# Score tiles on VectorE from the first slots on: 139 tiles instead of 94, with borrowed buffers and projections laid out by need

## The chip, the cores and the metric

The kernel runs on one core of one Trainium2 chip. The metric is the device time of one execution in microseconds (us). Executions of one kernel on one chip usually agree within 0.3%. All runs quoted are "fast" (none was over 1.5% above the fastest run of its kernel). Engine names in the profile: PE is TensorE's matmuls, PEld its weight loads, DVE is VectorE, ACT is ScalarE, POOL is GpSimd.

## The reference

```python
def reference(A_x, A_wqkv, A_w_phi, A_wo, B_x, B_wqkv, B_wo, gate_w):
    x = A_x                                            # 1 x 2048 x 512, 32 heads of 16
    g = sigmoid((x * gate_w).sum(-1, keepdims=True))
    a = linear_attention(x, A_wqkv, A_w_phi, A_wo)     # feature maps by softmax over 16
    b = softmax_attention(x, B_wqkv, B_wo)             # full 2048 x 2048 scores per head
    return g * a + (1 - g) * b
# ... (cut: the two blocks in full)
```

The softmax block needs 32 x 2048 x 2048 exponentials. Cut into tiles of 128 x 512 these are 2048 tiles. The linear block ("A" in names) is much smaller, and runs in the gaps.

## The kernel before

The program is a list of operations with planned durations and priorities. A list scheduler in the kernel's own Python lays them out once, at build time; each engine then executes its fixed order, and semaphores hold the dependences. One *slot* is three score tiles in three of the eight accumulation banks. ScalarE exponentiates all three, or two of them while VectorE does the third by a bit trick and a cubic (six operations). Two sets of three banks alternate, one bank holds the attention output, and one bank (`bM`) serves everything else. A *projection* is the matmuls that compute a piece of Q, K, V or the like into `bM`; the *drain* is the copy out of the bank afterwards, mostly by VectorE, and only then is `bM` free again. *Value products* multiply the exponentials by V.

```python
D_FROM, D_MID, D_RATE = 200, 420, (0.14, 0.25)    # VectorE tiles per slot: 0, then 0.14, then 0.25
# ... (cut)
def add_qk(j):                                    # scores of slot j
    def fn(e):
        if op.full > 0.3:                         # a dummy matmul ahead of the scores
            e.matmul(psS[:, 512 * base:512 * (base + 1)], lhsT=ident[:], rhs=WoA[:, 0, :], start=True, stop=True)
        for m, t in enumerate(ts):
            ins = qk_mm(e, t, psS[:, 512 * (base + m):512 * (base + m + 1)])
# ... (cut)
def add_exp(j):                                   # ScalarE: 1536 or 1024 columns
    op = P.add("act", ..., lambda e: e.activation(Ebuf[:, j % ERING, 0:512 * n],
        psS[:, 512 * base:512 * (base + n)], ACTF.Exp, bias=EBIAS, scale=ESCALE), ...)
# ... (cut) in the scheduler: PE work that the layout thinks PE owes, to keep it active
if op.name[:2] == "qk" and debt > self.inslot and t > 240.0:
    op.full = 0.42                                # this score group gets its dummy
```

When PE would otherwise have nothing to do and `bM` is free, the layout also puts "filler" dummies there. Dummies compute nothing; they keep PE active.

The softmax here doesn't subtract the row's maximum and nothing guards it: scores larger than these inputs give would overflow.

Of the kernel before, what the change touches and what calls it, by code (L numbers as in the profile page):

```python
# [13 lines left out]
S = 2048  # L14
# [19 lines left out]
DLAG = 10  # L34
D_FROM = 200
D_MID = 420
D_RATE = (0.14, 0.25)
ERING = 8
LAT = 0.12
# [38 lines left out]
class Plan:  # L78
# [37 lines left out]
    def layout(self):  # L116
# [16 lines left out]
        while left:  # L133
# [26 lines left out]
            for e in ENGINES:  # L160
# [39 lines left out]
                if e == "pe":  # L200
                    if op.name[:2] == "qk" and debt > self.inslot and t > 240.0:
                        op.full = 0.42
                        op.dur += 0.28
                    debt = max(debt - op.full, -0.2)
# [89 lines left out]
def _build(ctx, nc, A_x, A_wqkv, A_w_phi, A_wo, B_wqkv, B_wo, gate_w, out):  # L294
# [22 lines left out]
    phiK = sb([128, 8, 1024], name="phiK")  # L317
    Ebuf = sb([128, ERING, 1536], name="E")
    Pf = sb([128, 2, D], F32, name="Pf")
# [185 lines left out]

    def q_fill(r, qc, prio, banks=None, first=False):
        f, mm = fill(prio, proj([W_B[:, t, 128 * r:128 * (r + 1)] for t in range(KT)],
                                [xT[:, t, NQ * qc:NQ * (qc + 1)] for t in range(KT)]), ["wbq" if r else "wbq0"] + xk(qc), banks,
                     name=f"Q{r}.{qc}")
        for par in range(2):  # L510
            dst = qz[:, qc % 2, 2 * r + par, :]
            if first and par == 0:
                fn = lambda e, ap, dst=dst: e.activation(dst, ap, ACTF.Copy, scale=pmask[:, 0:1])
            else:
                fn = lambda e, ap, dst=dst, par=par: e.tensor_scalar(dst, ap, pmask[:, par:par + 1], None,  # L515
                                                                     op0=ALU.mult)
            e1 = drain(f, mm, "act" if first and par == 0 else "dve", 0.69, prio, fn, reads=["pmask"],
                       writes=[("q", qc % 2, 2 * r + par)], name=f"Qe{r}.{qc}.{par}", last=(par == 1),
                       after=[e1] if par == 1 else ())


    def d_rate(j):
        return 0.0 if j < D_FROM else D_RATE[0] if j < D_MID else D_RATE[1]

# [58 lines left out]
    for act, _ in slots:  # L583
        for t in act:
            last_act[t[0]] = t
    d_index = {j: n for n, (j, _) in enumerate(tiles_d)}
    ND = len(tiles_d)
    vfree = vAf[:, 0:8192].bitcast(F32).rearrange("p (n c) -> p n c", c=1024)
    I32 = mybir.dt.int32
    dT = [vfree[:, 0, :], vfree[:, 1, :]]  # L590
    dM, dU = vfree[:, 2, :], vfree[:, 3, :]
    dE = [W_B[:, t, D:3 * D] for t in range(KT)]

    exp_ops = [None] * NS
    pv_last = []
    d_wait = []

# [7 lines left out]
    def add_qk(j):  # L605
# [19 lines left out]
        if j == 1:  # L625
            op.take = [bS[3], bS[4], bS[5]]
        if j == 60:
            op.deps += P.writer["WoA"]
# [4 lines left out]
    def add_d(j, bank):  # L633

        n = d_index[j]
        bt, half = (n // 2) % 2, n % 2
        be = (n // 2) % 4
        free = (va_free + kv_mm) if n < 2 else ()
        P.add("dve", 0.72, -45, lambda e: e.tensor_scalar(  # L639
            dT[bt].bitcast(I32)[:, 512 * half:512 * half + 512], bank, EXPB, 0.0, op0=ALU.add, op1=ALU.max),  # L640
            reads=[("S", j % 2)], writes=[("dT", bt, half)], after=free, name=f"D1.{n}")
        if half == 0 and n + 1 < ND:
            return
        w = 512 * (half + 1)
        keys = [("dT", bt, h) for h in range(half + 1)]
        t, m, u = dT[bt][:, 0:w], dM[:, 0:w], dU[:, 0:w]
        P.add("dve", 0.75 * w / 1024, -20, lambda e: e.tensor_scalar(  # L647
            m.bitcast(I32), t.bitcast(I32), 0x007FFFFF, 0x3F800000, op0=ALU.bitwise_and, op1=ALU.bitwise_or),
            reads=keys, writes=["dM"], name=f"D2.{n}")
        P.add("dve", 0.75 * w / 1024, -20, lambda e: e.tensor_single_scalar(  # L650
            t.bitcast(I32), t.bitcast(I32), 0x7F800000, ALU.bitwise_and), reads=keys + ["dM"], writes=keys,
            name=f"D3.{n}")
        P.add("dve", 1.25 * w / 1024, -20, lambda e: e.scalar_tensor_tensor(u, m, C2, m, op0=ALU.add, op1=ALU.mult),  # L653
              reads=["dM"], writes=["dU"], name=f"D4.{n}")
        P.add("dve", 1.25 * w / 1024, -20, lambda e: e.scalar_tensor_tensor(u, u, C1, m, op0=ALU.add, op1=ALU.mult),  # L655
              reads=["dM", "dU"], writes=["dU"], name=f"D5.{n}")
        P.add("dve", 1.25 * w / 1024, -20, lambda e: e.scalar_tensor_tensor(  # L657
            dE[be][:, 0:w], u, C0, t, op0=ALU.add, op1=ALU.mult), reads=["dU"] + keys, writes=[("dE", be)],
            name=f"D6.{n}")

# [19 lines left out]
    def add_pv(j):  # L680
# [4 lines left out]
        for b, mts in parts.items():  # L685
# [7 lines left out]
            for x in list(d_wait):  # L693
                jd, n, t = x
                if t[0] != b or (b, t[1]) not in pv_started:
                    continue
                if last or (jd + DLAG <= j and t[1] not in heads):
                    d_wait.remove(x)
                    heads.append(t[1])
                    work.append((t, dE[(n // 2) % 4][:, 512 * (n % 2):512 * (n % 2) + 512], False))  # L700
                    if ("dE", (n // 2) % 4) not in reads:
                        reads.append(("dE", (n // 2) % 4))
            for t, _, _ in work:
# [12 lines left out]
            op.full = 0.21  # L716
            pv_last.append(op)
            if j == 0:
                op.take = [bO]
            if first:  # L720
                op.margin = 1.0
            if last:
                assert not [x for x in d_wait if x[2][0] == b]
                add_norm(b, op)
        if dt:
            d_wait.append((j, d_index[j], dt))

# [170 lines left out]
    def q_rest(i, prio):  # L898
# [7 lines left out]
        for rnd in range(2):  # L906
# [10 lines left out]
                  writes=[("dr", b, rnd)], name=f"nb{i}.{rnd}")  # L917
            P.add("dve", 0.38, -3, lambda e, dr=dr: e.tensor_scalar(dr, dr, g128[:, i:i + 1], None, op0=ALU.mult),
                  reads=[("dr", b, rnd), "g128"], writes=[("dr", b, rnd)], name=f"nc{i}.{rnd}")
# [36 lines left out]
    for r in range(1, KT):  # L956
        q_fill(r, 0, 57.0 * r - 15)
        for c in range(QC):
            k_fill(r, c, 57.0 * r - 14 + 6 * c)
            v_fill(r, c, 57.0 * r - 13 + 6 * c)  # L960
    gate()
# [17 lines left out]
    for j in range(NS):  # L979
        add_exp(j)  # L980
        if j + 2 < NS:
            add_qk(j + 2)
        add_pv(j)
        b1 = slots[j][0][-1][0]
        while q_next < NB and q_next // 8 >= 1 and q_next // 2 * 2 - 8 < b1:
            q_fill(q_next % 8 // 2, q_next // 8, 20.0 * q_next - 30)
            q_next += 2
    for j in (NS - 2, NS - 1):
        exp_ops[j].rel = [bS[3 * (j % 2) + m] for m in range(3)]

    P.idle = (bM, 0.05, lambda e: e.matmul(psM[:], lhsT=ident[:], rhs=WoA[:, 0, :], start=True, stop=True),  # L991
# [35 lines left out]
```

## Time and profile before

938.24 us median of 3 runs (937.41 to 938.62) when the prediction was made.

Lines of the page of the kernel before: busy time (share) and instructions by engine; busy tenths in 40 slices; the chain that ended last.

```profile
PE 810.6 (86%) x5807; PEld 253.5 (27%) x5908; DVE 595.1 (64%) x927; ACT 913.2 (97%) x720; POOL 142.0 (15%) x131
...
DVE  2436565457454787777856765476776776766774
ACT  6999999999999999999999999999999999999996
...
PEclk9999999999989999899999999999999999999999
...
ACT 91%; PE 6%; DVE 3%; issue 0%
```

Groups of instructions of the kernel before, ScalarE alone, shapes kept apart (busy us, mean ns of one | idle before).

```profile
L664 ACT ACTIVATE E_t<-psS 128x1536 bf16<-128x1536 f32 x588 | 815.7, 1572 | 7.9 <-PE psS L601 7.6
L664 ACT ACTIVATE E_t<-psS 128x1024 bf16<-128x1024 f32 x95 | 104.7, 1102 | 0.6 <-PE psS L601 0.6
L857 ACT ACTIVATE EA_t<-Dd_t 128x1024 bf16<-128x1024 bf16 x32 | 40.4, 1263 | 0.0
```

ScalarE is the bound: busy 97%, 91% of the chain. The recorded durations of successive exponentials overlap, so the useful number is the *pitch*, start to start. Reading the starts one by one, an undisturbed 1536-wide exponential has a pitch of 1330 ns, a 1024-wide one of 903, the linear block's (EA_t) of 946. "Idle before" (8.5 us for these two groups) shows less than half of the waiting, 19.7 us by pitch: the rest lies inside the records. I therefore use an account of my own throughout: the span is the head (to the first exponential), plus the sum of these undisturbed pitches, plus the excess of each real pitch over its undisturbed one, plus the tail. The excess is split into what lies within 1.5 us of a stretch where the clock records show half speed, what follows a short (1024-wide) exponential, and the rest. For the kernel before: 10.9 + 897.3 + (11.2 + 5.2 + 3.3) + 9.3 = 937.2 us.

### The profile page before, as it was taken

How to read it: one execution, taken by the hardware profiler on the slowest of the kernel's cores; microseconds unless marked ns; L12 is line 12 of the kernel's file. 1: busy time of each engine (PE TensorE's matmuls, PEld its weight loads, DVE VectorE, ACT ScalarE, POOL GpSimd, SP SyncE). 2: the span in 40 equal slices, each digit the busy share in tenths (PEclk: the TensorE clock that was granted, in tenths of full speed). 3: DMA queues.
4: the chain of work that ended last, by engine and by line, in shares of the span. 5: the costliest groups of instructions: out<-in, count | busy, mean ns of one | idle time of the engine just before them, and what ended most of it. 6: DMA issues, size and time to landing. Idle time of an engine off the chain costs nothing.

```text
span 937.2 us, 13684 instructions
## 1 busy us (share of the span) xinstructions
PE 810.6 (86%) x5807; PEld 253.5 (27%) x5908; DVE 595.1 (64%) x927; ACT 913.2 (97%) x720; POOL 142.0 (15%) x131
## 2 busy tenths in 40 slices
PE   8887888887888888888788888888999998899998
PEld 3232323322322222222222222222222222222222
DVE  2436565457454787777856765476776776766774
ACT  6999999999999999999999999999999999999996
POOL 5004334325321221400401200000000000000000
PEclk9999999999989999899999999999999999999999
DMA  7500000000000000000000000000000000000000
GB/s 147 124 2 1 1 1 1 1 1 1 1 7 12 1 7 1 1 2 1 1 1 1 18 7 1 1 1 1 1 1 1 17 6 1 1 1 1 1 1 23
DMA packets 18956, 9.28 MB, mean 10 GB/s; under 512 B 13264, under 2 KB 18896, under 8 KB 18896
## 3 DMA queue, kind: packets, MB, share of 16 engines
q1 hardware_dynamic: 16928, 8.00, 3.5%
q8 instruction: 46, 0.75, 0.3%
q10 hardware_dynamic: 1584, 0.39, 0.2%
q0 software_dynamic: 384, 0.02, 0.1%
q14 instruction: 14, 0.11, 0.0%
HBM read 3.69 MB, written 2.10 MB: 6 GB/s over the span
## 4 chain that ended last, share of the span: by engine, by line
ACT 91%; PE 6%; DVE 3%; issue 0%
ACT E_t L664 88%; ACT EA_t L857 3%; PE psS L601 1%; PE psO L677 1%; PE psM L479 1%; PE psS L619 1%; PE psM L395 1%; DVE stat_t L861 0%; PE psM L991 0%; DVE qz_t L515 0%; DVE rd_t L736 0%; DVE Wp_t L825 0%; DVE Tf_t L731 0%; DVE vA_t L647 0%; DVE Pf_t L842 0%
## 5 line engine op out<-in xcount | busy, mean ns | idle before, releaser
L664 ACT ACTIVATE E_t<-psS 128x1536 bf16<-128x1536 f32 (+1 forms) x683 | 890.3, 1507 | 8.5 <-PE psS L601 8.2
L601 PE MATMUL psS<-qz_t,kTB_t 32*128 32x512 bf16 x2048 | 272.7, 391 | 47.3 <-ACT E_t L664 38.5
L677 PE MATMUL psO<-E_t,vaug_t 128*32 128x512 bf16 (+1 forms) x1954 | 270.4, 398 | 1.0 <-ACT E_t L664 0.4
L619 PE MATMUL psS<-WoA_t,ident_t 128*128 128x512 bf16 x244 | 97.5, 399 | 51.2 <-ACT E_t L664 46.6
L639 DVE TENSOR_SCALAR vA_t<-psS 128x512 int32<-128x512 f32 x94 | 64.6, 687 | 113.2 <-PE psS L601 113.2
L601 PEld LDWEIGHTS psS<-qz_t,kTB_t 32*128 32x128 bf16 x2048 | 66.5, 91 | 239.9 <-ACT E_t L664 155.8
L677 PEld LDWEIGHTS psO<-E_t,vaug_t 128*32 128x32 bf16 (+1 forms) x1954 | 64.9, 93 | 154.4 <-issue 138.1
L991 PE MATMUL psM<-WoA_t,ident_t 128*128 128x512 bf16 x278 | 89.4, 385 | 2.0 <-issue 1.9
L851 POOL TENSOR_TENSOR Dd_t<-Pf_t,stat_t 128x512 bf16<-128x512 f32 x32 | 33.8, 1057 | 242.7 <-DVE stat_t L846 232.9
L619 PEld LDWEIGHTS psS<-WoA_t,ident_t 128*128 128x128 bf16 x274 | 26.5, 97 | 123.2 <-ACT E_t L664 115.1
L655 DVE SCALAR_TENSOR_TENSOR vA_t<-vA_t 128x1024 f32<-128x1024 f32 x47 | 57.1, 1216 | 0.8
L657 DVE SCALAR_TENSOR_TENSOR WB_t<-vA_t 128x1024 bf16<-128x1024 f32 x47 | 57.1, 1215 | 0.8
L653 DVE SCALAR_TENSOR_TENSOR vA_t<-vA_t 128x1024 f32<-128x1024 f32 x47 | 57.0, 1213 | 0.0
L842 DVE COPY Pf_t<-psM 128x512 f32<-128x512 f32 x32 | 21.9, 685 | 43.3 <-PE psM L479 41.3
L861 DVE TENSOR_REDUCE stat_t<-EA_t 128x64 f32<-128x1024 bf16 x32 | 38.7, 1212 | 15.2 <-ACT EA_t L857 15.1
L865 POOL TENSOR_TENSOR phiQ_t<-EA_t,stat_t 128x1024 bf16<-128x1024 bf16 x16 | 31.4, 1967 | 81.9 <-DVE stat_t L863 81.9
L479 PE MATMUL psM<-Wp_t,xT_t 128*128 128x512 bf16 x115 | 36.0, 384 | 6.3 <-DVE vA_t L834 3.4
L857 ACT ACTIVATE EA_t<-Dd_t 128x1024 bf16<-128x1024 bf16 x32 | 40.4, 1263 | 0.0
L865 POOL TENSOR_TENSOR phiK_t<-EA_t,stat_t 128x1024 bf16<-128x1024 bf16 x16 | 30.8, 1928 | 53.7 <-DVE stat_t L863 46.0
L479 PE MATMUL psM<-xT_t,WB_t 128*128 128x512 bf16 x107 | 34.0, 396 | 4.5 <-issue 1.3
L677 PE MATMUL psO<-WB_t,vaug_t 128*32 128x512 bf16 (+1 forms) x94 | 37.3, 396 | 0.0
L647 DVE TENSOR_SCALAR vA_t<-vA_t 128x1024 int32<-128x1024 int32 x47 | 34.3, 730 | 1.2
(102 smaller groups left out, 581.0 us busy)
## 6 DMA issues: line engine op xcount, KB each, us to landing
out_dram<-WvA_t SPq DMA_DIRECT2D x16, 128.0 KB, 1.7
WB_t<-in_B_wqkv_dram SPq DMA_DIRECT2D x3, 384.0 KB, 4.3
Dd_t<-in_A_x_dram SPq DMA_DIRECT2D x4, 128.0 KB, 3.4
WvA_t<-in_A_wqkv_dram SPq DMA_DIRECT2D x1, 512.0 KB, 5.3
WoA_t<-in_A_wo_dram SPq DMA_DIRECT2D x1, 512.0 KB, 6.2
WoB_t<-in_B_wo_dram SPq DMA_DIRECT2D x1, 512.0 KB, 6.6
WB_t<-in_B_wqkv_dram ACTq DMA_DIRECT2D x3, 128.0 KB, 3.8
xT_t<-in_A_x_dram SPq DMA_TRANSPOSE x12, 4.0
```

The costliest lines, as they stand in the source:

```text
L479: return [lambda e, ap, i=i: e.matmul(ap, lhsT=lhs[i], rhs=rhs[i], start=(i == 0), stop=(i == len(lhs) - 1)) for i in range(len(lhs))]
L601: return e.matmul(bank, lhsT=kT_B[32 * i:32 * i + 32, hg // 2, 128 * kt:128 * (kt + 1)], rhs=qz[32 * i:32 * i + 32, (b // 8) % 2, hg, :], ...
L619: e.matmul(psS[:, 512 * base:512 * (base + 1)], lhsT=ident[:], rhs=WoA[:, 0, :], start=True, stop=True)
L639: P.add("dve", 0.72, -45, lambda e: e.tensor_scalar(dT[bt].bitcast(I32)[:, 512 * half:512 * half + 512], bank, EXPB, 0.0, op0=ALU.add, op1 ...
L653: P.add("dve", 1.25 * w / 1024, -20, lambda e: e.scalar_tensor_tensor(u, m, C2, m, op0=ALU.add, op1=ALU.mult), reads=["dM"], writes=["dU"] ...
L655: P.add("dve", 1.25 * w / 1024, -20, lambda e: e.scalar_tensor_tensor(u, u, C1, m, op0=ALU.add, op1=ALU.mult), reads=["dM", "dU"], writes= ...
L657: P.add("dve", 1.25 * w / 1024, -20, lambda e: e.scalar_tensor_tensor(dE[be][:, 0:w], u, C0, t, op0=ALU.add, op1=ALU.mult), reads=["dU"] + ...
L664: op = P.add("act", 0.07 + 0.000833 * 512 * n, 0.0, lambda e: e.activation(Ebuf[:, j % ERING, 0:512 * n], psS[:, 512 * base:512 * (base + ...
L677: return e.matmul(psO[32 * i:32 * i + w, :], lhsT=vaug[:, kt, VW * h:VW * h + w], rhs=rhs, start=start, stop=stop, tile_position=(0, 32 * ...
L857: ex = P.add("act", 1.2, -4, lambda e: e.activation(EA[:, b, :], Dd[:, b, :], ACTF.Exp), reads=[("D", b, 0), ("D", b, 1)], writes=[("EA", ...
L865: P.add("pool", 2.0, prio, lambda e: e.tensor_tensor(dst.rearrange("p (g f) -> p g f", f=DH), e3, stat[:, b, 1, :].unsqueeze(2).to_broadca ...
L991: P.idle = (bM, 0.05, lambda e: e.matmul(psM[:], lhsT=ident[:], rhs=WoA[:, 0, :], start=True, stop=True), P.writer["WoA"][0])
```

## The change

Its intent: let VectorE take score tiles also in the first 200 slots. The buffers of the late tiles are still in use then, so an early pool borrows those of the linear block's query pass, which has to wait for the last early tile. More tiles late as well. Projections of K, V and Q are laid out by when they are needed, and dummies inside score groups may come from 60 us on, not 240. Cut to the core:

```diff
-D_FROM = 200
-D_MID = 420
-D_RATE = (0.14, 0.25)
-ERING = 8
+D_RATE = ((14, 0.15), (196, 0.0), (222, 0.17), (420, 0.31))
+D_SWITCH = 210
+ERING = 7
@@ scheduler
-                    if op.name[:2] == "qk" and debt > self.inslot and t > 240.0:
+                    if op.name[:2] == "qk" and debt > self.inslot and t > 60.0:
@@ buffers of VectorE tiles
+    dp_early = DPool("a", 512, [f32(phiQ[:, 0, :]), f32(phiQ[:, 1, :])], f32(qtf[:, 0, :]), f32(qtf[:, 1, :]),
+                     [oA[:, 0, :], oA[:, 1, :]] + [Ebuf[:, ERING, 512 * k:512 * k + 512] for k in range(3)], ())
+    dp_late = DPool("b", 1024, [vfree[:, 0, :], vfree[:, 1, :]], vfree[:, 2, :], vfree[:, 3, :],
+                    [W_B[:, t, D:3 * D] for t in range(KT)], (va_free, kv_mm))
@@ projections
-        q_fill(r, 0, 57.0 * r - 15)
+        q_fill(r, 0, 34.0 * r - 20)
         for c in range(QC):
-            k_fill(r, c, 57.0 * r - 14 + 6 * c)
-            v_fill(r, c, 57.0 * r - 13 + 6 * c)
+            k_fill(r, (c - 1) % QC, 34.0 * r - 19 + 3 * c)
+        for c in range(QC):
+            v_fill(r, c, 34.0 * r - 7 + 4 * c)
@@ (cut: planned durations, a cheaper denominator scaling, and the query pass's wait for the early tiles)
```

The number of slots stays 683. By the instructions of the program, 94 VectorE tiles become 139 (27 early, 112 late), and dummies go from 274 in score groups and 308 fillers to 403 and 90.

More of the change, by code (lines that the diff above doesn't have):

```diff
@@ L317, in _build @@
     phiK = sb([128, 8, 1024], name="phiK")
-    Ebuf = sb([128, ERING, 1536], name="E")
+    Ebuf = sb([128, ERING + 1, 1536], name="E")
     Pf = sb([128, 2, D], F32, name="Pf")
@@ L504, in v_fill, with q_fill @@
             dst, ap.rearrange("p (i h d) -> p i h d", i=4, d=DH)), writes=[("v", r, c)], name=f"Ve{r}.{c}")
-    def q_fill(r, qc, prio, banks=None, first=False):
+    def q_fill(r, qc, prio, banks=None, first=False, after=()):
         f, mm = fill(prio, proj([W_B[:, t, 128 * r:128 * (r + 1)] for t in range(KT)],
                                 [xT[:, t, NQ * qc:NQ * (qc + 1)] for t in range(KT)]), ["wbq" if r else "wbq0"] + xk(qc), banks,
-                     name=f"Q{r}.{qc}")
+                     name=f"Q{r}.{qc}", after=after)
         for par in range(2):
@@ L522, in d_rate @@
     def d_rate(j):
-        return 0.0 if j < D_FROM else D_RATE[0] if j < D_MID else D_RATE[1]
+        return max([(j0, r) for j0, r in D_RATE if j0 <= j] + [(-1, 0.0)])[1]
     NB = QC * 8
@@ L585, in _build, with __init__, place, f32 @@
             last_act[t[0]] = t
-    d_index = {j: n for n, (j, _) in enumerate(tiles_d)}
-    ND = len(tiles_d)
-    vfree = vAf[:, 0:8192].bitcast(F32).rearrange("p (n c) -> p n c", c=1024)
-    I32 = mybir.dt.int32
-    dT = [vfree[:, 0, :], vfree[:, 1, :]]
-    dM, dU = vfree[:, 2, :], vfree[:, 3, :]
-    dE = [W_B[:, t, D:3 * D] for t in range(KT)]
+    I32 = mybir.dt.int32
+    class DPool:
+        def __init__(self, tag, w, t, m, u, e, free):
+            self.tag, self.w, self.t, self.m, self.u, self.e, self.free = tag, w, t, m, u, e, free
+            self.per = w // 512
+            self.n, self.ops = 0, []
+        def place(self, n):
+            k = n // self.per
+            return k % len(self.t), n % self.per, k % len(self.e)
+    def f32(ap):
+        return ap.bitcast(F32)
+    vfree = vAf[:, 0:8192].bitcast(F32).rearrange("p (n c) -> p n c", c=1024)
+    qtf = phiQT[:].rearrange("p b g q -> p b (g q)")
+    dp_early = DPool("a", 512, [f32(phiQ[:, 0, :]), f32(phiQ[:, 1, :])], f32(qtf[:, 0, :]), f32(qtf[:, 1, :]),
+                     [oA[:, 0, :], oA[:, 1, :]] + [Ebuf[:, ERING, 512 * k:512 * k + 512] for k in range(3)], ())
+    dp_late = DPool("b", 1024, [vfree[:, 0, :], vfree[:, 1, :]], vfree[:, 2, :], vfree[:, 3, :],
+                    [W_B[:, t, D:3 * D] for t in range(KT)], (va_free, kv_mm))
+    d_place = {}
+    for j, _ in tiles_d:
+        dp = dp_early if j < D_SWITCH else dp_late
+        d_place[j] = (dp, dp.n)
+        dp.n += 1
     exp_ops = [None] * NS
     pv_last = []
-    d_wait = []
+    d_wait, early_pv, early_last = [], [], []
     def qk_mm(e, t, bank):
@@ L626, in add_qk @@
             op.take = [bS[3], bS[4], bS[5]]
-        if j == 60:
+        if j == 35:
             op.deps += P.writer["WoA"]
@@ L633, in add_d @@
     def add_d(j, bank):
-        n = d_index[j]
-        bt, half = (n // 2) % 2, n % 2
-        be = (n // 2) % 4
-        free = (va_free + kv_mm) if n < 2 else ()
-        P.add("dve", 0.72, -45, lambda e: e.tensor_scalar(
-            dT[bt].bitcast(I32)[:, 512 * half:512 * half + 512], bank, EXPB, 0.0, op0=ALU.add, op1=ALU.max),
-            reads=[("S", j % 2)], writes=[("dT", bt, half)], after=free, name=f"D1.{n}")
-        if half == 0 and n + 1 < ND:
+        dp, n = d_place[j]
+        bt, half, be = dp.place(n)
@@ new lines, in add_d, with add @@
+        free = sum(dp.free, []) if n < 2 * dp.per else ()
+        def add(dur, prio, fn, reads, writes, name):
+            dp.ops.append(P.add("dve", dur, prio, fn, reads=reads, writes=[(dp.tag,) + k for k in writes],
+                                after=free, name=f"{name}.{j}"))
+        add(0.70, -45, lambda e: e.tensor_scalar(
+            dp.t[bt].bitcast(I32)[:, 512 * half:512 * half + 512], bank, EXPB, 0.0, op0=ALU.add, op1=ALU.max),
+            [("S", j % 2)], [("T", bt, half)], "D1")
@@ L643, in add_d @@
+        if half < dp.per - 1 and n + 1 < dp.n:
             return
         w = 512 * (half + 1)
-        keys = [("dT", bt, h) for h in range(half + 1)]
-        t, m, u = dT[bt][:, 0:w], dM[:, 0:w], dU[:, 0:w]
-        P.add("dve", 0.75 * w / 1024, -20, lambda e: e.tensor_scalar(
-            m.bitcast(I32), t.bitcast(I32), 0x007FFFFF, 0x3F800000, op0=ALU.bitwise_and, op1=ALU.bitwise_or),
-            reads=keys, writes=["dM"], name=f"D2.{n}")
-        P.add("dve", 0.75 * w / 1024, -20, lambda e: e.tensor_single_scalar(
-            t.bitcast(I32), t.bitcast(I32), 0x7F800000, ALU.bitwise_and), reads=keys + ["dM"], writes=keys,
-            name=f"D3.{n}")
@@ L653, in add_d @@
-        P.add("dve", 1.25 * w / 1024, -20, lambda e: e.scalar_tensor_tensor(u, m, C2, m, op0=ALU.add, op1=ALU.mult),
-              reads=["dM"], writes=["dU"], name=f"D4.{n}")
-        P.add("dve", 1.25 * w / 1024, -20, lambda e: e.scalar_tensor_tensor(u, u, C1, m, op0=ALU.add, op1=ALU.mult),
-              reads=["dM", "dU"], writes=["dU"], name=f"D5.{n}")
-        P.add("dve", 1.25 * w / 1024, -20, lambda e: e.scalar_tensor_tensor(
-            dE[be][:, 0:w], u, C0, t, op0=ALU.add, op1=ALU.mult), reads=["dU"] + keys, writes=[("dE", be)],
-            name=f"D6.{n}")
+        f1, f2 = 0.17 + 0.53 * w / 1024, 0.17 + 1.06 * w / 1024
@@ new lines, in add_d @@
+        tk = [("T", bt, h) for h in range(half + 1)]
+        rt = [(dp.tag,) + k for k in tk]
+        rm, ru = [(dp.tag, "M")], [(dp.tag, "U")]
+        t, m, u = dp.t[bt][:, 0:w], dp.m[:, 0:w], dp.u[:, 0:w]
+        add(f1, -20, lambda e: e.tensor_scalar(m.bitcast(I32), t.bitcast(I32), 0x007FFFFF, 0x3F800000,
+                                               op0=ALU.bitwise_and, op1=ALU.bitwise_or), rt, [("M",)], "D2")
+        add(f1, -20, lambda e: e.tensor_single_scalar(t.bitcast(I32), t.bitcast(I32), 0x7F800000, ALU.bitwise_and),
+            rt + rm, tk, "D3")
@@ L661, in add_exp @@
+        add(f2, -20, lambda e: e.scalar_tensor_tensor(u, m, C2, m, op0=ALU.add, op1=ALU.mult), rm, [("U",)], "D4")
+        add(f2, -20, lambda e: e.scalar_tensor_tensor(u, u, C1, m, op0=ALU.add, op1=ALU.mult), rm + ru, [("U",)], "D5")
+        add(f2, -20, lambda e: e.scalar_tensor_tensor(dp.e[be][:, 0:w], u, C0, t, op0=ALU.add, op1=ALU.mult),
+            ru + rt, [("E", be)], "D6")
     def add_exp(j):
@@ L693, in add_pv @@
             for x in list(d_wait):
-                jd, n, t = x
+                jd, t = x
                 if t[0] != b or (b, t[1]) not in pv_started:
@@ L699, in add_pv @@
                     heads.append(t[1])
-                    work.append((t, dE[(n // 2) % 4][:, 512 * (n % 2):512 * (n % 2) + 512], False))
-                    if ("dE", (n // 2) % 4) not in reads:
-                        reads.append(("dE", (n // 2) % 4))
+                    dp, n = d_place[jd]
+                    _, half, be = dp.place(n)
+                    work.append((t, dp.e[be][:, 512 * half:512 * half + 512], False))
+                    if (dp.tag, "E", be) not in reads:
+                        reads.append((dp.tag, "E", be))
+                    if dp is dp_early:
+                        early_pv.append(j)
             for t, _, _ in work:
@@ L717, in add_pv @@
             pv_last.append(op)
+            if early_pv and early_pv[-1] == j:
+                early_last[:] = [op]
             if j == 0:
@@ L722, in add_pv @@
             if last:
-                assert not [x for x in d_wait if x[2][0] == b]
+                assert not [x for x in d_wait if x[1][0] == b]
                 add_norm(b, op)
         if dt:
-            d_wait.append((j, d_index[j], dt))
+            d_wait.append((j, dt))
     def add_norm(b, pv):
@@ L917, in q_rest @@
                   writes=[("dr", b, rnd)], name=f"nb{i}.{rnd}")
-            P.add("dve", 0.38, -3, lambda e, dr=dr: e.tensor_scalar(dr, dr, g128[:, i:i + 1], None, op0=ALU.mult),
+            P.add("dve", 0.2, -3, lambda e, dr=dr: e.tensor_tensor(dr, dr, g128[:, i:i + 1].to_broadcast([128, 16]),
+                                                                   ALU.mult),
                   reads=[("dr", b, rnd), "g128"], writes=[("dr", b, rnd)], name=f"nc{i}.{rnd}")
@@ L985, in _build @@
         while q_next < NB and q_next // 8 >= 1 and q_next // 2 * 2 - 8 < b1:
-            q_fill(q_next % 8 // 2, q_next // 8, 20.0 * q_next - 30)
+            q_fill(q_next % 8 // 2, q_next // 8, -0.5, after=[exp_ops[j]])
             q_next += 2
@@ L989, in _build @@
         exp_ops[j].rel = [bS[3 * (j % 2) + m] for m in range(3)]
+    for op in P.ops:
+        if op.name in ("phi0.0", "phi0.1", "Te0", "Te1", "nd0.0", "nd0.1", "nd1.0", "nd1.1"):
+            op.deps = op.deps + dp_early.ops[-1:] + early_last
     P.idle = (bM, 0.05, lambda e: e.matmul(psM[:], lhsT=ident[:], rhs=WoA[:, 0, :], start=True, stop=True),
```

## The prediction

> **What bounds the kernel now.** ScalarE. In the page's engine table ACT is busy 913.2 of 937.2 us (97%), DVE 595.1 (64%). The chain of waits is 88% the score exponential. By shape, the groups of instructions give 588 exponentials of 1536 columns and 95 of 1024. In the timeline an undisturbed 1536-wide one is followed by the next after 1330 ns, a 1024-wide one after 903 to 928 ns, so a tile taken off ScalarE saves 0.40 to 0.43 us. The Trainium skill, "ScalarE: Activation LUTs", What ACT_TABLE_LOAD costs, gives 0.833 ns per column (427 ns for 512) and an overlap of successive ACTIVATEs; the trace agrees (recorded duration 1572 ns, pitch 1330).
>
> Beyond that work the chain holds about 10.9 us before the first exponential, 9.2 us from the last one's start to the end, and some 18 us of excess pitch. About 11 us of that lies where the clock records show half speed (seven of eight such stretches of 3.4 or 6.8 us, all before 565 us). The rest is mostly 70 to 160 ns at half of the 1024-wide slots: the next scores come too late after a short exponential.
>
> **What the change does.** Slots stay 683; VectorE tiles go from 94 to 139 (27 early, 112 late), so 45 exponentials shrink from 1536 to 1024 columns: 45 x 0.41 = 18.5 us off ScalarE, all on the critical path.
>
> It adds VectorE work. A late pair costs 6.46 us by the durations shown (2x0.687+0.730+0.708+3x1.215), so 9 more pairs cost 58 us. An early tile, all passes at 512 columns, is estimated from them at 3.6 us; 27 cost 97 us. VectorE goes from 595 to about 745 us, 81% of the new span. By the order of instructions and these durations, slots 440 to 600 come to about 47 to 53 us of VectorE per 40 slots against 48 to 51 of ScalarE: nearly level. PE keeps its real work; dummy matmuls go from 308 fillers and 274 inside score groups to 90 and 403, the latter from 60 us on instead of 240. They delay the scores by one matmul but keep the clock up.
>
> **The sum.** 938.2 - 18.5 = 919.7. Added: 45 more short slots with the same small wait, about +4; VectorE queueing where it is level, about +3. Removed: fewer half-clock stretches before 240 us (three now, with about 4 us of stall) and less stall from fills, about -6. Result 920.5 us, 8 in 10 between 911 and 932. Chances: faster by over 2% (below 919.5) 0.43, within 2% 0.53, slower 0.04.
>
> **What would show it.** ACT busy falls to about 895 us, with 543 wide and 140 narrow exponentials at unchanged pitch. DVE busy rises to 735 to 755 us. The wait of the exponential for scores stays under about 15 us in total; the score matmuls' waits on the first VectorE pass (0.8 us now) grow, but stay below 8 us. Clock records: at most six half-speed stretches, few before 240 us.
>
> **What would make it wrong.** (a) VectorE lags in slots 440 to 600: the first pass, which frees the score bank, comes late, PE then ScalarE wait, and half of the gain is lost. (b) The in-slot dummies make each short slot wait 0.2 us, not 0.07. (c) Drains stuck behind VectorE tiles starve PE and bring more half-clock stretches. (d) Upwards: the clock never drops, and up to 11 us of stall goes as well; then about 913.

## The result, and the profile after

The changed kernel took 926.51 us median of 4 runs (926.42 to 928.06), the kernel before 938.4 (937.41 to 938.62) beside it. The ratio is 0.9879, 95% interval 0.9862 to 0.9896. That is 1.2% faster: within the 2% to which the prediction gave 0.53, inside the predicted range, but 6 us short of the point.

The same lines of the page, changed kernel:

```profile
PE 794.1 (86%) x5717; PEld 249.3 (27%) x5819; DVE 725.0 (78%) x1152; ACT 896.5 (97%) x720; POOL 152.5 (16%) x131
...
DVE  2477687778886577688677967899999989898893
ACT  6999999999999999999999989999999999999996
...
PEclk9999999989999989997999979999999999999999
...
ACT 84%; PE 11%; DVE 5%; issue 0%
```

And its groups of instructions, ScalarE alone:

```profile
L685 ACT ACTIVATE E_t<-psS 128x1536 bf16<-128x1536 f32 x543 | 755.9, 1501 | 10.6 <-PE psS L621 10.1
L685 ACT ACTIVATE E_t<-psS 128x1024 bf16<-128x1024 f32 x140 | 151.1, 1079 | 0.8 <-PE psS L621 0.8
L884 ACT ACTIVATE EA_t<-Dd_t 128x1024 bf16<-128x1024 bf16 x32 | 35.7, 1114 | 0.0
```

The work did move: 45 exponentials are narrower, ACT is busy 16.7 us less, DVE 130 us more. But the chain now runs 11% through PE instead of 6%, and the clock row dips in four slices where it dipped in two, at other places. The account:

| us | before | after | difference |
|---|---|---|---|
| head and tail | 20.2 | 21.5 | +1.3 |
| undisturbed pitches | 897.3 | 878.1 | -19.2 (45 x 0.427) |
| excess near half-speed stretches | 11.2 | 11.1 | -0.1 |
| excess behind a short exponential | 5.2 | 7.3 | +2.1 |
| other excess | 3.3 | 6.7 | +3.4 |
| span | 937.2 | 924.7 | -12.5 |

So the gain is the pitch of 45 tiles, and a third of it is spent again. Half speed took 41.0 us in 8 stretches before, and 44.4 us in 7 after. (The 1 us in the head is not of the change: other kernels below with the same first instructions have heads between 10.5 and 11.9 us.)

**What precedes a drop of the clock.** All stretches of half speed in these two traces begin on a grid of 3.413 us, and last one to four such windows. The Trainium skill, "TensorE: Matmul & The Clock Gate", What's actually happening, describes this: a clock gate with two states, set by a free-running activity window of 3413 ns; the records here agree (stretches of 3413, 6827 and 13653 ns, mean clock 0.5 in them and 1 elsewhere). So I looked at the window that ends where a drop begins. Busy time by engine in stretches of the changed kernel: the first three end at a drop, the last is an ordinary one.

```profile
core 0: us, PE busy (x) PEld busy (x) DVE busy (x) ACT busy (x) POOL busy (x), PEclk, DMA share, GB/s
...
423.33:426.74 3.41, 1.66 (x12) 0.40 (x11) 3.28 (x6) 3.41 (x4) 0.80 (x1) 1.00 0.00 0
529.14:532.55 3.41, 1.54 (x13) 0.58 (x14) 3.41 (x6) 3.41 (x3) 0.00 (x0) 1.00 0.00 0
542.79:546.20 3.41, 2.15 (x25) 0.86 (x22) 3.41 (x5) 3.31 (x3) 1.93 (x1) 1.00 0.00 0
640.00:643.41 3.41, 3.41 (x23) 0.99 (x21) 3.26 (x4) 3.41 (x3) 0.00 (x0) 1.00 0.00 0
```

The same view of the kernel before: two windows that end at a drop, and an ordinary one.

```profile
86.74:90.15 3.41, 2.12 (x19) 0.59 (x18) 3.29 (x5) 3.41 (x5) 2.75 (x3) 1.00 0.02 5
...
383.70:387.11 3.41, 1.16 (x10) 0.39 (x8) 3.41 (x5) 3.41 (x4) 0.00 (x0) 1.00 0.00 0
...
640.00:643.41 3.41, 2.91 (x23) 0.76 (x21) 3.41 (x6) 3.41 (x4) 0.00 (x0) 1.00 0.00 0
```

In the windows shown that end at a drop PE was busy 34 to 63%, in the ordinary ones 85 and 100%. Some matmul records are missing (403 weight loads but 348 matmuls of the dummies, for example), so for the count below I filled them in from the weight loads (how this is done moves the first two rows: as recorded, without filling, they are 60 windows with 48 drops and 184 with 41, and the last row 3398 with none). Over the traces of all fourteen kernels, windows at full speed in which PE was busy

| busy share of a 3.413 us window | windows | followed by a drop |
|---|---|---|
| under 0.60 | 49 | 45 |
| 0.60 to 0.70 | 119 | 44 |
| 0.70 and over | 3373 | 0 |

The kernel before has 8 windows under 0.65, the changed one 9: the change did not touch what makes the clock fall. What PE is doing in such a window, in the timeline of the changed kernel (start, us, engine, line, operation; in brackets the idle time before it):

```profile
start us, us, engine line op out<-in xcount [idle before <-releaser]
...
423.25 1.46 ACT L685 ACTIVATE E_t<-psS 128x1536 bf16<-128x1536 f32 x1
423.35 0.10 PEld L479 LDWEIGHTS psM<-Wp_t,xT_t 128*128 128x128 bf16 x1 [0.23 <-issue]
423.35 0.39 PE L479 MATMUL psM<-Wp_t,xT_t 128*128 128x512 bf16 x1
...
424.58 1.08 ACT L884 ACTIVATE EA_t<-Dd_t 128x1024 bf16<-128x1024 bf16 x1
...
424.77 0.39 PE L639 MATMUL psS<-WoA_t,ident_t 128*128 128x512 bf16 x1 [1.03 <-ACT E_t L685]
...
425.09 0.39 PE L621 MATMUL psS<-qz_t,kTB_t 32*128 32x512 bf16 x3
...
427.05 0.61 PE L639 MATMUL psS<-WoA_t,ident_t 128*128 128x512 bf16 x1 [1.03 <-ACT E_t L685]
...
427.60 0.61 PE L621 MATMUL psS<-qz_t,kTB_t 32*128 32x512 bf16 x3
```

ScalarE inserts one of the linear block's exponentials (EA_t). That holds the next score exponential back by 0.95 us, so PE, which is ahead, waits 1.03 us for ScalarE to free a bank, once before 424.77 and once more before 427.05. Meanwhile it runs nothing else: its order is fixed, and `bM` is taken by a projection (L479) whose last matmul ended at 423.74 and which VectorE, busy with other work, drained only at 436.99, so that there is no filler either. The clock then drops at 426.74; the same matmuls take 0.61 us instead of 0.39, a slot with its dummy no longer fits into 1330 ns, and exponentials follow each other at 1626 ns, one even after 2487. In six of the seven stretches of the changed kernel such an EA_t exponential began 2 to 5 us before the drop. That is no accident of their number: of its windows at full speed after 60 us, 29 have an EA_t exponential at that place, and in 8 of these PE was busy under 0.65; of the 118 others up to 600 us, in one.

### The profile page after: what moved, and what is told of

The parts are those of the page before. It is cut to its first block, busy times and chain, and to the rows that moved or that the text cites. A ratio compares the mean times of both kernels' runs of the same rounds, so it can differ in the third digit from the quotient of the medians.

```text
span 924.7 us, 13749 instructions
## 1 busy us (share of the span) xinstructions
PE 794.1 (86%) x5717; PEld 249.3 (27%) x5819; DVE 725.0 (78%) x1152; ACT 896.5 (97%) x720; POOL 152.5 (16%) x131
## 4 chain that ended last, share of the span: by engine, by line
ACT 84%; PE 11%; DVE 5%; issue 0%
ACT E_t L685 81%; ACT EA_t L884 3%; PE psS L621 3%; PE psO L698 2%; PE psS L639 2%; PE psM L479 1%; PE psM L395 1%; DVE vA_t L662 0%; PE psM L1023 0%; DVE vA_t L677 0%; DVE phiQT_t L930 0%; DVE vA_t L673 0%; DVE vA_t L678 0%; DVE stat_t L888 0%; DVE WB_t L679 0%
## 5 line engine op out<-in xcount | busy, mean ns | idle before, releaser
L685 ACT ACTIVATE E_t<-psS 128x1536 bf16<-128x1536 f32 (+1 forms) x683 | 868.8, 1415 | 11.4 <-PE psS L621 10.9
L639 PE MATMUL psS<-WoA_t,ident_t 128*128 128x512 bf16 x348 | 140.7, 404 | 67.7 <-ACT E_t L685 63.2
L662 DVE TENSOR_SCALAR vA_t<-psS 128x512 int32<-128x512 f32 x112 | 76.8, 685 | 37.0 <-PE psS L621 35.8
L639 PEld LDWEIGHTS psS<-WoA_t,ident_t 128*128 128x128 bf16 x403 | 38.9, 97 | 181.8 <-ACT E_t L685 161.0
L677 DVE SCALAR_TENSOR_TENSOR vA_t<-vA_t 128x1024 f32<-128x1024 f32 x56 | 71.7, 1280 | 0.0
L679 DVE SCALAR_TENSOR_TENSOR WB_t<-vA_t 128x1024 bf16<-128x1024 f32 x56 | 68.1, 1216 | 0.3
L678 DVE SCALAR_TENSOR_TENSOR vA_t<-vA_t 128x1024 f32<-128x1024 f32 x56 | 67.9, 1212 | 0.3
L698 PE MATMUL psO<-WB_t,vaug_t 128*32 128x512 bf16 (+1 forms) x112 | 43.2, 395 | 0.0
L675 DVE TENSOR_SCALAR vA_t<-vA_t 128x1024 int32<-128x1024 int32 x56 | 40.6, 724 | 0.6
L673 DVE TENSOR_SCALAR vA_t<-vA_t 128x1024 int32<-128x1024 int32 x56 | 40.3, 720 | 0.4
L881 POOL TENSOR_TENSOR Dd_t<-stat_t,Pf_t 128x512 bf16<-128x512 f32 x32 | 36.3, 1136 | 20.6 <-DVE stat_t L875 20.6
L479 PE MATMUL psM<-Wp_t,xT_t 128*128 128x512 bf16 x117 | 36.8, 385 | 3.2 <-DVE oA_t L953 0.5
L479 PE MATMUL psM<-xT_t,WB_t 128*128 128x512 bf16 x110 | 34.7, 393 | 4.3 <-DVE qz_t L515 1.6
L758 DVE STREAM_TRANSPOSE Tf_t<-psO 128x512 f32<-128x512 f32 x32 | 22.8, 712 | 18.5 <-PE psO L698 18.0
```

The lines of the kernel that those rows point to most:

```text
L479: return [lambda e, ap, i=i: e.matmul(ap, lhsT=lhs[i], rhs=rhs[i], start=(i == 0), stop=(i == len(lhs) - 1)) for i in range(len(lhs))]
L662: add(0.70, -45, lambda e: e.tensor_scalar(dp.t[bt].bitcast(I32)[:, 512 * half:512 * half + 512], bank, EXPB, 0.0, op0=ALU.add, op1=ALU.ma ...
L673: add(f1, -20, lambda e: e.tensor_scalar(m.bitcast(I32), t.bitcast(I32), 0x007FFFFF, 0x3F800000, op0=ALU.bitwise_and, op1=ALU.bitwise_or), ...
L675: add(f1, -20, lambda e: e.tensor_single_scalar(t.bitcast(I32), t.bitcast(I32), 0x7F800000, ALU.bitwise_and), rt + rm, tk, "D3")
L677: add(f2, -20, lambda e: e.scalar_tensor_tensor(u, m, C2, m, op0=ALU.add, op1=ALU.mult), rm, [("U",)], "D4")
L678: add(f2, -20, lambda e: e.scalar_tensor_tensor(u, u, C1, m, op0=ALU.add, op1=ALU.mult), rm + ru, [("U",)], "D5")
```

## The experiments

Theory A: the tiles pay nearly their pitch everywhere; what is missing is that half-speed stretches, caused by idle PE windows, stayed. Rivals: B, VectorE (8 to 9 tenths busy from 600 us on) lags, so that the late tiles pay nothing; D, the dummies in front of the scores delay them; L, the layout of the projections gains and the tiles give it back. In the table, clock is the range of the mean granted clock over the timed runs, the rest is of the profiled run and in us; "half" is the length of half-speed stretches within the span.

| kernel | tiles | median (range) | clock | half | pitches | excess: half | behind short | other |
|---|---|---|---|---|---|---|---|---|
| before | 94 | 938.4 (937.4-943.2) | 0.973-0.984 | 41.0 | 897.3 | 11.2 | 5.2 | 3.3 |
| changed | 139 | 926.5 (926.4-928.1) | 0.971-0.976 | 44.4 | 878.1 | 11.1 | 7.3 | 6.7 |
| e1 | 94 | 939.5 (931.8-942.2) | 0.975-0.993 | 47.8 | 897.3 | 13.4 | 4.3 | 4.7 |
| e2 | 118 | 933.3 (932.5-933.7) | 0.982-0.984 | 34.1 | 887.1 | 11.8 | 7.6 | 3.7 |
| e3 | 112 | 927.6 (926.8-928.3) | 0.993-0.994 | 13.7 | 889.7 | 3.6 | 6.6 | 5.3 |
| e4 | 139 | 936.2 (931.2-943.5) | 0.940-0.963 | 78.5 | 878.1 | 24.6 | 6.8 | 4.3 |
| e5 | 139 | 918.2 (916.6-921.6) | 0.991-0.998 | 3.4 | 878.1 | 0.8 | 8.0 | 8.0 |
| e6 | 139 | 925.0 (922.4-931.2) | 0.971-0.989 | 20.5 | 878.1 | 8.3 | 5.5 | 7.9 |
| e7 | 94 | 940.6 (937.8-941.6) | 0.978-0.991 | 23.9 | 897.3 | 8.7 | 5.3 | 6.3 |
| e8 | 139 | 985.5 (980.7-987.6) | 0.964-0.976 | 47.8 | 878.1 | 47.8 | 8.8 | 22.6 |
| e9 | 139 | 927.8 (923.5-929.0) | 0.972-0.983 | 47.8 | 878.1 | 14.3 | 3.1 | 11.3 |
| e10 | 94 | 936.7 (933.2-937.7) | 0.993-0.998 | 13.7 | 897.3 | 5.0 | 5.5 | 7.4 |
| e11 | 158 | 980.6 (976.1-984.3) | 0.920-0.942 | 146.8 | 870.0 | 51.6 | 6.6 | 19.5 |
| e12 | 112 | 933.4 (933.3-935.2) | 0.985-0.989 | 23.9 | 889.7 | 7.2 | 6.6 | 8.1 |

For before, the median is that of the first four runs, while ranges are over all calls; its medians in the calls of e1 to e4, e5 to e8 and e9 to e12 were 939.06, 939.49 and 938.72 us. All twelve experiments gave correct outputs.

### e1: the tile rates of before

```diff
-D_RATE = ((14, 0.15), (196, 0.0), (222, 0.17), (420, 0.31))
-D_SWITCH = 210
+D_RATE = ((200, 0.14), (420, 0.25))
+D_SWITCH = 0
```

> The changed kernel with the tile rates of before (94 VectorE tiles, none early), so only the layout of the projections, the ring of 7, dummies inside score groups from 60 us and the cheaper denominator scaling remain. Theory A (the layout and the earlier dummies were to remove stall, and did not, since the half-clock stretches stay): 936 to 940 us, half-clock stall again 9 to 13 us. Theory L (the layout does save its few us, and the tiles give it back): 931 to 935 us.

939.48 us, ratio 0.9963 (0.9907 to 1.002): the layout alone gains nothing that can be told from noise, as theory A says; L falls as the explanation of the median. Its excess outside half speed is 9.0 us, against 8.5 before. More telling is the spread. The same program took 931.8 us in the run whose mean clock was 0.993 and 942.1 us in both runs at 0.975: 10 us, presumably from where the free-running window happened to fall, which no run sets on purpose. Within e1, e4, e6 and e9 a straight line through the runs gives 4.8 to 5.7 us per 0.01 of mean clock (e1: 5.7, e9: 5.1); within e5, e7, e8, e10 and e11 it gives 2.8 (e7) to 7.6 (e10).

### e2: early tiles alone, and e3: late tiles alone

```diff
 # e2
+D_RATE = ((14, 0.15), (196, 0.0), (222, 0.14), (420, 0.25))
 # e3
+D_RATE = ((222, 0.17), (420, 0.31))
```

> The changed kernel with the late rates of before (0.14 from slot 222, 0.25 from 420) and the early tiles kept: 119 narrow exponentials, 24 more than before, worth 24 x 0.427 = 10.2 us by pitch. Theory A (every tile pays nearly its full pitch wherever it is; what is missing is the clock): 928 to 931 us. Theory B (VectorE is nearly full in the late slots, so the extra late tiles pay nothing): the same time as the whole change, 925 to 928 us.

> The changed kernel without early tiles, late rates kept: 113 narrow exponentials, 18 more than before, worth 7.7 us by pitch. Theory A: 930 to 933 us. Theory B: 936 to 939 us, as before.

e2 took 933.29 us, later than either theory said; e3 took 927.64, earlier than either said, and as good as the whole change with 27 tiles fewer. Theory B falls, though not by the median of e3, most of which is the clock. The late tiles pay by the account below, and e2 against the changed kernel shows it: 21 more late tiles made it 6.8 us faster, at a clock that is no higher. Why e3 beats what its tiles are worth is in the account. Against e1, its pitches are 7.7 us less and its excess outside half speed 2.9 us more, a net 4.8; the other 10 us are half-speed excess (3.6 instead of 13.4). (These are the profiled runs, 928.3 and 942.2 us; the medians lie 12 us apart.) Only the rates differ between e1 and e3, so 18 more tiles moved the whole static order, and fewer idle windows came out of it. Against e1 in the same way, e2's tiles are worth 10.2 - 2.3 = 7.9 us and those of the whole change 19.2 - 5.0 = 14.2.

### e4: dummies in score groups from 240 us again

```diff
-                    if op.name[:2] == "qk" and debt > self.inslot and t > 60.0:
+                    if op.name[:2] == "qk" and debt > self.inslot and t > 240.0:
```

> The changed kernel with dummy matmuls inside score groups only from 240 us, as before (46 fewer). If the earlier dummies hold the clock up: more half-clock stretches before 240 us than the one of the changed kernel, 928 to 932 us. If they only delay the scores: 923 to 926 us. If neither matters: within 1 us of the changed kernel's 926.5.

936.19 us: 46 dummies fewer cost 10 us, more than I expected. The clock rows of the page, e4 first, then e3:

```profile
PEclk9999989986999989799997997999999999999999
```

```profile
PEclk9999999999999999999999899999999999999999
```

e4 has 78.5 us at half speed: 37.5 us before 240 us, where the changed kernel has 6.8, and 41.0 after it, where that has 37.5. So the added half speed lies where the dummies were taken out. Its excess outside half speed is 11.1 us, 2.9 us less than the changed kernel's 14.0. So the first two sentences of the expectation hold at once: a dummy in front of the scores delays them a little (D), and without it the clock falls (A), which costs far more.

### e5: four dummies where ScalarE does an EA_t exponential

```diff
+                if e == "act":
+                    onact = op.name
@@
-                        op.full = 0.42
-                        op.dur += 0.28
+                        k = 4 if onact[:2] == "ex" and onact[:3] != "exp" else 1
+                        op.full = 0.21 + 0.21 * k
+                        op.dur += 0.06 + 0.22 * k
@@ in the score group: as many dummies as op.full says (17 groups got four; 472 dummies instead of 403)
```

> The changed kernel, with four dummy matmuls instead of one inside a score group that is laid out while ScalarE does a linear block's exponential (the place where PE idles 1.2 to 1.9 us just before the clock drops). Theory A (half clock follows PE idleness there, and costs 11 us): half-clock time falls from 44 us to under 25, time 918 to 923 us. Theory D (dummies in front of the scores cost as much as they save): 925 to 929 us. If the drops have another cause: no change in half-clock time.

918.24 us, ratio 0.9777 (0.9743 to 0.9812) to before: theory A's range. The page of e5:

```profile
PE 783.6 (86%) x5750; PEld 251.3 (27%) x5851; DVE 726.3 (79%) x1152; ACT 894.1 (98%) x720; POOL 154.6 (17%) x131
...
PEclk9999999999999999999999999999999999999999
```

One window at half speed is left in the span (half-speed excess 0.8 us instead of 11.1), with the same tiles, and with DVE and PE as busy as in the changed kernel (79 and 86%, from 78 and 86%). Of the windows at full speed with an EA_t exponential 2 to 5 us before their end, 2 of 25 are now under 0.65 (8 of 29 in the changed kernel), and none was followed by a drop (six there). This is the missing part of the gain, and the fastest kernel.

### e6: dummies behind the value products

```diff
-                    if op.name[:2] == "qk" and debt > self.inslot and t > 60.0:
+                    if op.name[:2] == "pv" and op.more and t > 60.0:
+                        k = (1 if debt > 0.1 else 0) + (1 if debt > 0.36 else 0)
+                        # ... and 3 more while ScalarE does an EA_t exponential
@@ behind the value products of the slot (zer is a tile of zeros)
+                for _ in range(round((op.full - 0.21) / 0.21)):
+                    ins = e.matmul(psO[:], lhsT=zer[:], rhs=WoA[:, 0, :], start=False, stop=False, ...)
```

> The changed kernel, with the dummy matmuls taken out of the score groups and put behind the value products instead (zero weights, added onto the output bank, so they change nothing), about as many, and up to three more where ScalarE does the linear block's exponential. They no longer delay the scores. Theory A: half-clock time under 25 us and 917 to 922 us. Theory D (the dummy in front of the scores is what makes the waits outside the half-clock stretches, 14 us in all): these waits fall to under 9 us too, then 912 to 918 us. If matmuls with zero weights do not hold the clock: many more stretches, over 940 us.

924.97 us. Half-speed time fell to 20.5 us, so matmuls with zero weights do count as activity. The windows say it more directly: in 41 windows at full speed PE was busy 0.70 or more, but would have been under 0.60 without the zero-weight matmuls, and no drop followed any of them. But the waits outside half speed stayed (13.4 us, from 14.0): taking the dummy off the scores' path took 1.8 us off "behind short" and put 1.2 us onto "other". As a way out it is worse than e5.

### e7: the dummies of e5 in the kernel before

> The kernel before with the four dummies of e5 and nothing else. Theory A: the clock's loss is independent of the change, so it falls here too, from 938.5 to 931 to 936 us at a higher granted clock. If the change's VectorE work is what brings the half-clock stretches: no gain, 937 to 940 us.

940.64 us, no gain: theory A's expectation failed here. Half-speed time did fall (41.0 to 23.9 us), but its excess only from 11.2 to 8.7 us, and the waits outside grew by 3.1. One difference is to be seen in the traces: in the kernel before, an EA_t exponential began 2 to 5 us before only three of the eight drops, against six of seven in the changed kernel. The four dummies removed just these: e7 has none of them, but as many others as before, five. So it seems that they mend the drops behind an EA_t exponential and no others; in e10 and e12 below, with the same dummies, none of four and one of four drops lie behind one.

### e8: many more dummies behind the value products

```diff
-        self.idle, self.rate, self.inslot = None, 0.57, 0.12
+        self.idle, self.rate, self.inslot = None, 0.68, 0.12
```

> As e6, with the layout's target for PE activity raised from 0.57 to 0.68, which gives 807 dummies behind the value products instead of 476. Theory A: half-clock time under 10 us, 911 to 918 us. If so many dummies crowd PE and delay scores: over 922 us at a clock near 1.

985.53 us, the worst. A dummy sits in an operation of higher priority than projections and output products, so these pile up. Waits of e8:

```profile
ACT E_t L693 <- PE psO L748: 31.6, 4, 29.5
```

ScalarE once stood still for 29.5 us (around 870 us) while PE and VectorE went through output products, transposes and drains that were due earlier. That idle stretch then ran at half speed itself.

### e9: e5 without dummies behind a short exponential

```diff
-                        k = 4 if onact[:2] == "ex" and onact[:3] != "exp" else 1
+                        k = 4 if onact[:2] == "ex" and onact[:3] != "exp" else 0 if short else 1
```

> As e5, but no dummy inside a score group that is laid out while ScalarE does a 1024-wide exponential (332 groups with dummies instead of 421). In the trace of e5, 6.4 us of the waits outside half clock lie at groups with one dummy behind a short exponential, and only 1.2 us where the first VectorE pass ended after the exponential. Theory D (there the dummy is what comes too late): excess pitch behind narrow exponentials falls from 8.0 to under 3.5 us, 912 to 916 us while the clock stays above 0.99. If the dummy is not the cause: 917 to 920 us. If these dummies hold the clock: clock under 0.99 and over 920 us.

927.84 us at a clock of 0.972 to 0.983. The excess behind short exponentials fell from 8.0 to 3.1 us: theory D is right about those waits. And the third sentence came true as well: without these dummies half speed is back, 47.8 us of it, as its clock row shows.

```profile
PEclk9999999999989999999889989999999899998999
```

These waits are part of what holding the clock costs.

### e10 and e12: e1 and e3 with the dummies of e5

> e1 (94 VectorE tiles, layout of the changed kernel) with the four dummies of e5. It measures what the 45 tiles are worth when the clock is held in both. Nominal worth 19.2 us by pitch, less some 7 us of further waits that e5 has over e1 outside half clock. Theory A: clock 0.99 or better, 928 to 934 us, 12 to 16 us above e5's 918. If the dummies bring nothing at these rates (as in e7): 936 to 941 us.

> e3 (late rates of the change, no early tiles: 112 tiles) with the four dummies of e5. With the clock held, the 27 early tiles are worth 11.5 us by pitch less their waits. Theory A: 923 to 927 us, 6 to 9 us above e5. If early tiles are worth nothing: 917 to 920 us.

e10 took 936.72 us: its clock is held (0.993 to 0.998), but the time lies in the range that I gave for no effect. Its excess outside half speed is 12.9 us against e1's 9.0, so here the dummies cost 3.9 us and gave 8.4. The medians of e10 and e5 lie 936.7 - 918.2 = 18.5 us apart, but e10's clock is mostly 0.993. At the same clock of 0.998, one run of e10 took 933.2 us and two of e5 916.6 and 917.0: at a held clock the 45 tiles are worth some 16.4 us. The account says 19.2 - 3.1 = 16.1, the 3.1 being what e5 has over e10 in waits outside half speed. e12 took 933.36 us, above both expectations and slower than e3 (927.64): its half-speed time rose from 13.7 to 23.9 us, with 3.6 us more of excess there, and its waits outside by 2.8 us. So the dummies of e5 are no general cure. Each edit of the layout draws the idle windows anew, and in a kernel like e3 that had drawn well there was little to win: one of its three drops followed an EA_t exponential.

### e11: more tiles still

```diff
 # on top of e9
+D_RATE = ((14, 0.15), (196, 0.0), (222, 0.20), (420, 0.36))
```

> As e9, with late rates 0.20 and 0.36 instead of 0.17 and 0.31: 158 VectorE tiles, 19 more, worth 8.1 us by pitch. Theory B (VectorE at 92 to 96% from 600 to 800 us is the limit): the first passes come later than the exponentials, the waits grow by 8 us or more, and it is not faster than e9. If VectorE still has room: 5 to 8 us below e9.

980.56 us, 53 us slower than e9 with 19 more tiles. Its page, and its waits between 600 and 900 us:

```profile
PE 830.9 (85%) x5778; PEld 241.8 (25%) x5778; DVE 773.3 (79%) x1221; ACT 893.3 (91%) x720; POOL 154.9 (16%) x131
...
PEclk9999999999999999999999997777875799877999
```

```profile
ACT E_t L688 <- PE psS L624: 40.1, 53, 1.7
...
PEld psS L624 <- DVE vA_t L665: 5.9, 8, 2.2
...
PEld psS L642 <- DVE vA_t L665: 3.7, 6, 0.8
```

Here theory B is true at last: scores wait for VectorE's first pass over a bank (L665), PE idles, and the clock falls to 0.7 in slice after slice, 146.8 us at half speed in all. For comparison, who waited for that first pass in the whole of the changed kernel, and of the kernel before (us, times):

```profile
  PEld psS L639: 1.9, 5
  PE psS L621: 1.0, 2
  PEld psO L698: 0.9, 2
  PE psS L639: 0.6, 1
```

```profile
  PEld psM L907: 0.8, 1
  PE psS L601: 0.8, 2
```

The change stops just short of this edge. e11 stands on e9, which had already lost dummies; against it the 19 tiles cost 53 us: 37 us of half-speed excess, 12 of other excess, and 12 of a longer tail (21.2 us from the last exponential's start to the end, from 9.5), in which output products come that had been left undone, less 8 of pitch. Whether the fall would be as deep with the dummies kept was not tried.

## Why the prediction was right or wrong

- *ScalarE is the bound, and 45 tiles are worth 18.5 us on the critical path.* Right: 19.2 us (45 x 0.427), found whole in the account; waits take some of it back (e10). Its use of the Trainium skill, "ScalarE: Activation LUTs", What ACT_TABLE_LOAD costs, held: 0.833 ns per column gives 427 ns for 512 columns, and 1330 - 903 = 427.
- *Added waits of +4 and +3 us.* Right in size: +2.1 behind short exponentials and +3.4 elsewhere. Their causes were as named only in part: by the order of starts, in only 1 to 2 us of the changed kernel's 14.0 us outside half speed had VectorE's first pass ended after the exponential that frees the other banks. Behind short exponentials the cause is the dummy in front of the scores (e9: 8.0 us fell to 3.1); for the rest the cause was not shown.
- *Removed: fewer half-clock stretches before 240 us and less stall from fills, -6 us.* This is the step that failed. Before 240 us there was indeed one stretch instead of three, but four of 3.4 to 13.7 us came between 280 and 430, and the total rose from 41.0 to 44.4 us. The excess there stayed (11.2, 11.1). I counted dummies, 582 against 493, and did not ask in which windows PE would be idle; and I took it that earlier dummies only subtract stretches. They do hold the clock early (e4), but stretches follow single windows of 3.4 us with PE busy under 0.6 to 0.7, and the new order has as many of those as the old one. e1 shows that the projections' layout removed no stall either. With the half-speed excess nearly gone, e5 took 918 us, close to the 920.5 of the prediction's sum. The other terms were off by 1.5 us or less, so nearly the whole miss is this term, and it was the width of the range that held it.
- *Head and tail.* Not in the prediction: +1.3 us, scatter of the head.
- *What would show it.* ACT busy about 895 us: 896.5. 543 and 140 exponentials at unchanged pitch: yes. DVE 735 to 755 us: 725.0, since records of successive DVE operations overlap by some 0.08 us and I added up durations. Waits of the exponential under 15 us: 11.4 in the page's group. Waits on the first pass under 8 us: at most 3.5 by score groups. At most six half-speed stretches: seven.
- *What would make it wrong.* (a) did not occur here, but is what ends e11. (b) was too pessimistic: outside half speed 79 short slots with a dummy waited 5.7 us in all, 0.07 us each, as the prediction's sum had it. (c) is near the mark: in the stretch shown above, PE starves while `bM` waits 13 us for a drain and ScalarE does other work; but the stretches did not become more. (d) is what e5 made happen: predicted "about 913", measured 918, because its dummies add 2 us of waits.

What stays open: why some layouts draw few idle windows (e3) and others many (e1). The runs show that half speed follows from low windows; they do not give a rule for the layout that avoids them. e5 rests on four runs of one layout. Its clock is not safe either: the same trace, cut at twelve phases of the 3.413 us grid, has 0 to 5 windows under 0.60 outside its half-speed stretches (the kernel before: 0 to 6), and its own runs range from a clock of 0.998 and 916.6 us to 0.991 and 921.6.

## What to carry to other kernels

When an engine other than PE is the bound and PE is kept at full clock by dummies, a change of order can also be a change of the clock: judge a change by an account that separates undisturbed pitch, waits at full clock and waits at half clock, and compare kernels at like granted clock before believing a gain or a loss of 1%. Look for the single clock windows with PE idle, not at the mean activity, and put spare matmuls where the bounding engine goes away to other work. Work moved to a second engine paid here until that engine was nearly full; then it delayed its partner, the partner's clock fell, and 8 us of pitch cost 53 (e11 against e9), so stop short of that edge.

## What the Trainium skill lacked or had wrong

- "TensorE: Matmul & The Clock Gate", What's actually happening, says that the clock halves after an idle window of about 3.4 us, and HAM oscillation gives the rule "no PE-idle gaps >~3.4µs". Here far less was enough: the longest single idle gap in a window before a drop was 1.57 us in the two kernels compared and 2.33 over all fourteen (e9), and before four of the eight drops of the kernel before no gap was over 0.63 us. What told was the busy share of the window: under 0.60, 45 of 49 were followed by half speed, from 0.60 to 0.70, 44 of 119, from 0.70 up, none of 3373. The grid of 3413 ns and the two states are as the page says, and A second HAM failure mode tells of such micro-idling; a threshold is not in the page.
- The same page describes the phase of the free-running window as something that shifts the warm-up at the start. Here it seems to decide later stretches too: single executions of one program on one chip differed by 12 us (e4: 931.2 us at a clock of 0.963, 943.5 at 0.940), and one trace of the kernel before, cut at twelve phases, has 0 to 6 windows under 0.60. That the phase alone does it is inferred; no run set it.
- No page says whether matmuls with zero weights keep the clock up. They do: in e6 all dummies after 60 us but the fillers had zero weights, half-speed time was 20.5 us instead of 44.4, and no drop followed the 41 windows that these matmuls alone lifted from under 0.60 to 0.70 or more.
- "ScalarE: Activation LUTs", What ACT_TABLE_LOAD costs, gives about 93 ns of overlap between successive activations. Here the shortest records of 1536-wide exponentials are 1.44 us at a pitch of 1330 ns (an overlap of some 110 ns), and the mean record is 1572 ns in the kernel before, as a record also holds waiting. Busy times summed from records are therefore too long, and the pitch is what to count.
